# Expert weights in DRAM as quarters of 128 rows of 4 KB, and a spare 896-byte tile in the feed-forward stage

## The chip, the cores and the metric

The kernel runs on one core of one Trainium2 chip. The metric is the device time of the run in microseconds (us). All data are float32; the engines are TensorE (PE in the rows, PEld for its weight loads), VectorE (DVE), ScalarE (ACT), GpSimd (POOL) and SyncE (SP, which here issues most of the DMA transfers).

## The reference

Three layers follow each other on 8 x 3072 tokens of width 256: a spectral filter along the sequence, a mixture of 8 experts with one expert per token, and a dense feed-forward layer.

```
X = np.fft.rfft(x, axis=1)                       # x: (8, 3072, 256)
y = np.fft.irfft(X * (filt_r + 1j * filt_i)[None], n=3072, axis=1)
x = y.reshape(8 * 3072, 256)
logits = normalised(x) @ normalised(expert_emb).T / tau
expert_idx = argmax(logits); gate_w = softmax(logits)[expert_idx]
for e in range(8):                               # w1[e]: (256, 1024), w2[e]: (1024, 256)
    out[mask_e] = gate_w[mask_e] * (maximum(x[mask_e] @ w1[e], 0) @ w2[e])
h = out @ w_in                                   # (24576, 2048)
result = (h - tanh(h)) @ w_out
```

## The kernel before

**Stages.** The filter stage (`fft_phase`) computes the Fourier transforms as matrix products, batch after batch, routes each token, and scatters each token's row with GpSimd's indirect DMA (L393) into `region`, a DRAM buffer with one area per expert. The expert stage (`Moe`) then makes *visits*: one visit takes 384 or 256 consecutive rows of one expert's area through both matrices of that expert and writes the result to `x2T` in DRAM. The feed-forward stage (`ff_phase`, lines from L1200 on) comes last and fills more than half of the run.

**Visits.** The first visits (256 rows) run inside the filter stage, on experts that have enough rows by then. From visit `KV` on come the large ones (384 rows each), and then 13 small ones (256 rows each) for what is left over of each expert. One visit has four steps `b2`. In a step TensorE does 12 matmuls of the first matrix (`up`, L982) and, two steps late, 12 of the second (`down`, L1015); ScalarE and VectorE between them turn the first product into a high and a low part (`relu`, L992 and L993). Each engine works through its queue in order.

**Weights of an expert.** The matrices come in four *quarters* of 512 KB: quarters 0 and 1 are the two halves of `w1`, quarters 2 and 3 those of `w2`. One buffer, `raw`, holds one expert. In step `b2` of visit v the kernel first splits quarter `b2` of the next visit's expert into high and low parts (`split`: ScalarE L929, then VectorE or GpSimd L930), and then issues on SP the load of the same quarter for visit v+2 (`wload`, which calls `quarter`, L834 and L838). So a quarter that is reloaded has about one visit in which to arrive. From the second expert visit of the late part on, a load carries a condition (`cond=`) and moves nothing where the expert does not change; the split is done in every visit. The very first expert's weights go to a buffer of their own, `eraw`, inside the filter stage.

In `quarter` the source of a `w1` quarter is a view with three dimensions: 4 groups, 32 rows, 1024 values. The source of a `w2` quarter has 128 rows, 4 pieces of 256 values each:

```
wv = self.w1[bass.ds(e, 1)].rearrange("o (i k j) f -> (o k) i j f", i=4, k=2)
wv = self.w2[bass.ds(e, 1)].rearrange("o (b p) d -> (o p) b d", p=128)
```

**Rows of a visit.** SP also loads the visit's rows `y` in four parts (L896), reads the visit's numbers with small register loads (L823), and stores the result (L1028, L1029). GpSimd scales the rows (`rows`, L943 and L944), VectorE transposes them (L953), ScalarE and VectorE split them (L960, L961). L943 waits for the scatters of L393 that GpSimd issued before it.

**Buffers of the feed-forward.** `ff_phase` opens pools in the part of SBUF that the visits used; a tile there waits for the last user of the bytes that it takes. Its first small tile, `gones`, is filled by ScalarE (L1224) ahead of all of ScalarE's feed-forward work.

Of the kernel before, what the change touches and what calls it, by code (L numbers as in the profile page):

```python
# [16 lines left out]
F32 = mybir.dt.float32  # L17
# [9 lines left out]
D = 256  # L27
S = 3072
E = 8
FE = 1024  # L30
# [28 lines left out]
def flat(t):  # L59
    return t.rearrange("p a b -> p (a b)")  # L60
# [58 lines left out]
def fft_phase(tc, K, x, fr, fn, fi, emb, tau, region, ids, base, NB, CAP, moe):  # L119
# [3 lines left out]
    with ExitStack() as es:  # L123
# [208 lines left out]
        def route(b, g, Y, ss, L):  # L332
# [36 lines left out]

            P = L[:, 8:].rearrange("p a (b c) -> p (a b c)", b=4).rearrange("p (a b c) -> p a b c", a=2, b=8)  # L370

            def count():
                nc.tensor.matmul(P[:, 0], tri, ohv, start=True, stop=True)
                nc.tensor.matmul(P[:, 1], ones, ohv, start=True, stop=True)

            def place():

                inc = rp.tile([128, 8, 8], F32, name="inc", bufs=1)
                nc.vector.tensor_tensor_scan(flat(inc), flat(mask), flat(P[:, 1]), 0.0, op0=ALU.mult, op1=ALU.add)
                a = rp.tile([128, 8, 8], F32, name="a8", bufs=1)  # L380
                nc.vector.tensor_tensor(a, inc, P[:, 1], op=ALU.subtract)
                nc.vector.tensor_tensor(a, a, P[:, 0], op=ALU.add)
                nc.vector.tensor_tensor(a, a, bc(base), op=ALU.add)
# [376 lines left out]
class Moe:  # L760
# [68 lines left out]

    def quarter(self, q, e, **kw):  # L830

        if q < 2:
            wv = self.w1[bass.ds(e, 1)].rearrange("o (i k j) f -> (o k) i j f", i=4, k=2)
            self.tc.nc.sync.dma_start(self.raw[0][:, q], wv[q], **kw)  # L834
        else:
            wv = self.w2[bass.ds(e, 1)].rearrange("o (b p) d -> (o p) b d", p=128)
            b = slice(4 * q - 8, 4 * q - 4)
            self.tc.nc.sync.dma_start(self.raw[1][:, b], wv[:, b], **kw)  # L838

    def fetch(self, q):  # L840

# [364 lines left out]
def ff_phase(tc, x2T, ids, out, weights, mx, N, X0, fits, again):  # L1206

    nc = tc.nc
# [2 lines left out]
    NG = 8 * NT  # L1211
    with ExitStack() as es:
        P = lambda name, bufs, **kw: es.enter_context(tc.tile_pool(name=name, bufs=bufs, reuse_waits="tile", **kw))
        cp = P("gc", 1)
        beta = cp.tile([128, 1], F32, name="beta")
        nc.vector.memset(beta, BETA)
# [255 lines left out]
        for t in range(NT + 1):  # L1472
            for e, q in queue.items():
                seen = {}
                for n in table(t)[e].split():
                    i = seen[n] = seen.get(n, -1) + 1
# [14 lines left out]
        r = nc.values_load(bigi, min_val=0, max_val=1, skip_runtime_bounds_check_because="0 or 1")  # L1491
# [80 lines left out]
def moe_again(tc, region, w1, w2, x2T, ids, cnt, NA, N, CAP):  # L1572

    nc = tc.nc
    with ExitStack() as es:
        P = lambda name, bufs, **kw: es.enter_context(tc.tile_pool(name=name, bufs=bufs, **kw))
        p, hb = P("ag", 1), P("agb", 2)
        hp, op, dp = P("agh", 2, space=PSUM), P("ago", 2, space=PSUM), P("agd", 1, space=DRAM)
        zero = p.tile([128, RW], F32, name="zero")
        nc.vector.memset(zero, 0.0)  # L1580
        for i in range(TV // 128 * E):
            e, r = divmod(128 * i, TV)
            nc.sync.dma_start(region[e * CAP + r : e * CAP + r + 128], zero)
        sc = moe_schedule(tc, p, cnt, moe_numbers(tc, p, CAP, NA), CAP)
        table = dp.tile([128, 4], I32, name="table")
        nc.sync.dma_start(table, sc)
        NT = TV // 32
        with tc.For_i(0, N // TV + E - 1, 1) as v:
            line = p.tile([1, 4], I32, name="line")
            nc.sync.dma_start(line, table[bass.ds(v, 1)])  # L1590
            val = lambda k, top: nc.values_load(line[:, k : k + 1], engines=[SP], min_val=0, max_val=top,
                                                skip_runtime_bounds_check_because="the schedule stays inside")
            row, col, e = val(0, 8 * CAP - TV), val(1, N), val(2, E - 1)
            raw1 = p.tile([128, 2, FE], F32, name="raw1")
            raw2 = p.tile([128, 8, D], F32, name="raw2")
            wv = w1[bass.ds(e, 1)].rearrange("o (i k j) f -> (o k) i j f", i=4, k=2)
            for k in range(2):
                nc.sync.dma_start(raw1[:, k], wv[k])
            nc.sync.dma_start(raw2, w2[bass.ds(e, 1)].rearrange("o (b p) d -> (o p) b d", p=128))
            w1h, w1l = [p.tile([128, 2, FE], F32R, name=n) for n in ("w1h", "w1l")]  # L1600
            w2h, w2l = [p.tile([128, 8, D], F32R, name=n) for n in ("w2h", "w2l")]
            for r, h, l in ((raw1, w1h, w1l), (raw2, w2h, w2l)):
                nc.scalar.activation(h, r, AF.Copy)
                nc.vector.tensor_tensor(l, r, h.bitcast(F32), op=ALU.subtract)
            y = p.tile([128, NT, 68], F32, name="y")
            rv = region[bass.ds(row, TV)].rearrange("(t j) c -> j t c", j=32)
            for i, c in enumerate(QUARTERS):
                o = i % 2 * 2
                nc.sync.dma_start(y[32 * i : 32 * i + 32, :, o : o + 66], rv[:, :, c : c + 66])
            for q in (32, 96):  # L1610
                nc.gpsimd.tensor_copy(y[q : q + 32, :, 0:1], y[q : q + 32, :, 66:67])
            ys, yt = [p.tile([128, 2 * TV], F32, name=n) for n in ("ys", "yt")]
            nc.gpsimd.tensor_tensor(ys.rearrange("p (k t c) -> p t k c", k=2, c=32),
                                    y[:, :, 2:66].rearrange("p t (k c) -> p t k c", k=2),
                                    y[:, :, 0:1].unsqueeze(3).to_broadcast([128, NT, 2, 32]), op=ALU.mult)
            it, it2 = [p.tile([32, 32], I32, name=n) for n in ("it", "it2")]
            nc.vector.memset(it, 0)
            nc.vector.tensor_copy(it[:, :NT], y[:32, :, 1:2].bitcast(I32).rearrange("p t o -> p (t o)"))
            nc.vector.transpose(yt, ys)
            nc.vector.transpose(it2, it)  # L1620
            yh, yl = [p.tile([128, 2, TV], F32R, name=n) for n in ("yh", "yl")]
            nc.scalar.activation(flat(yh), yt, AF.Copy)
            nc.vector.tensor_tensor(flat(yl), yt, flat(yh).bitcast(F32), op=ALU.subtract)
            out = [op.tile([128, 512], F32, name="o")[:, :TV] for _ in range(2)]
            for fb in range(8):
                h = hp.tile([128, 512], F32, name="h")[:, :TV]
                c = slice(128 * fb, 128 * fb + 128)
                n = 0
                for k in range(2):
                    for a, b in ((w1h, yh), (w1h, yl), (w1l, yh)):  # L1630
                        nc.tensor.matmul(h, a[:, k, c], b[:, k], start=n == 0, stop=n == 5)
                        n += 1
                hh, hl = [hb.tile([128, TV], F32R, name=n) for n in ("hh", "hl")]
                nc.scalar.activation(hh, h, AF.Relu)
                nc.vector.scalar_tensor_tensor(hl, h, 0.0, hh.bitcast(F32), op0=ALU.max, op1=ALU.subtract)
                for d in range(2):
                    c = slice(128 * d, 128 * d + 128)
                    for n, (a, b) in enumerate(((w2h, hh), (w2h, hl), (w2l, hh))):
                        nc.tensor.matmul(out[d], a[:, fb, c], b, start=fb == 0 and n == 0, stop=fb == 7 and n == 2)
            x2 = p.tile([128, 2, TV], F32, name="x2")  # L1640
            for d in range(2):
                nc.scalar.activation(x2[:, d], out[d], AF.Copy)
            nc.sync.dma_start(x2T[:, bass.ds(col, TV)].rearrange("(k p) n -> p k n", p=128), x2)
            nc.sync.dma_start(ids[bass.ds(col, TV)].rearrange("(t j) -> t j", j=32), it2[:NT])
# [48 lines left out]
def arrange(x, filt_r, filt_i, moe_expert_emb, moe_tau, moe_w1, moe_w2, moe2_w_in, moe2_w_out):  # L1693
    mats, bins = dft_constants()
    c = np.ascontiguousarray
    a = dict(mats)
    a["x"] = c(x)
    a["fr"] = c(filt_r[bins[0]]).reshape(2 * N2, NP * D)
    a["fn"] = c(filt_r[S // 2 :])
    a["fi"] = c(filt_i[np.concatenate([bins[0, :, : NP // 2], bins[0, :, NP // 2 :]])]).reshape(NK, NP // 2 * D)  # L1700
    a["emb"] = c(moe_expert_emb)
    a["tau"] = np.asarray(moe_tau).reshape(1, 1)
    a["w1"] = c(moe_w1)
    a["w2"] = c(moe_w2)
    a["w_in"] = c(moe2_w_in).view(np.int64)
    a["w_out"] = c(moe2_w_out).view(np.int64)
    return a
# [15 lines left out]
```

## Time and profile before

| | |
|---|---|
| median of 3 runs | 3803.2 us (3803.08 to 3803.39) |
| the profiled execution, its own time | 3800.12 us |
| its span, first to last instruction | 3798.3 us |
| TensorE busy (matmuls) | 3684.9 us, 97% of the span |
| granted TensorE clock, mean | 0.987 of full speed |

The profiled execution took 1.8 us more than its span, and the median of the runs lies 3.1 us above it. The busy share is an average over three very different stages, so the rows below are taken stage by stage. "Granted clock" 1.00 is 2.4 GHz, 0.5 is 1.2 GHz.

### The profile page before, as it was taken

Reading aid. Unit: us, or ns where it says so; the run is one execution under the profiler, and the core shown is the slowest. Engines: PE = TensorE matmul, PEld = TensorE weight load, DVE = VectorE, ACT = ScalarE, POOL = GpSimd, SP = SyncE. Lnnn points to the kernel's source line nnn. Section 1 sums busy time; section 2 is a strip of 40 time slices with the busy share of each in tenths; the row PEclk is TensorE's granted clock in tenths of the full one; section 3 lists DMA queues with packets and bytes.
Section 4 is the critical chain, followed back from the end, with each engine's and each line's share of the span. In section 5 each row is a group of like instructions: output and inputs, shape, how many; then the busy total and the mean of one; then the engine's idle time right before and its main releaser. Section 6 shows DMA issues by size and latency. Waiting matters only on the chain.

```text
span 3798.3 us, 67513 instructions
## 1 busy us (share of the span) xinstructions
PE 3684.9 (97%) x23860; PEld 3348.8 (88%) x23860; DVE 2701.0 (71%) x5090; ACT 2536.1 (67%) x4327; POOL 2273.3 (60%) x1597
## 2 busy tenths in 40 slices
PE   6999889999999999989999999999999999999998
PEld 3666568999999999978899999999999999999997
DVE  4788885777887787647666666666666666676666
ACT  3566655455555555546777777777777777777775
POOL 2476666344344434435677777777777777777765
PEclk8999999999999999999999999999999999999999
DMA  8999864423332232440000000000000000000000
GB/s 258 300 296 295 267 183 143 104 56 82 84 81 81 70 94 58 110 122 26 29 25 27 23 29 23 29 23 28 24 29 23 23 29 27 25 23 29 25 28 18
DMA packets 295829, 308.49 MB, mean 81 GB/s; under 512 B 150193, under 2 KB 236346, under 8 KB 295482
## 3 DMA queue, kind: packets, MB, share of 16 engines
q1 hardware_dynamic: 232634, 199.37, 19.5%
q10 hardware_dynamic: 44416, 53.77, 4.3%
q0 software_dynamic: 18432, 50.95, 3.7%
q8 instruction: 190, 3.11, 0.3%
q14 instruction: 157, 1.29, 0.1%
HBM read 277.22 MB, written 127.41 MB: 107 GB/s over the span
## 4 chain that ended last, share of the span: by engine, by line
PE 85%; DMA 5%; DVE 5%; issue 2%; ACT 1%; POOL 1%; SPq 0%; POOLq 0%; ACTq 0%; DVEq 0%
PE h L1296 24%; PE po L1300 19%; PE h L982 12%; PE o L1015 12%; PE po L1301 10%; DMA raw<-in_w 3%; PE z L270 2%; PE z L255 2%; PE z L228 1%; PE z L297 1%; PE h L1281 1%; DVE u L262 1%; DVE v L261 1%; DVE v L260 1%; DMA region<-Y,pi 1%
## 5 line engine op out<-in xcount | busy, mean ns | idle before, releaser
L1362 POOL TENSOR_TENSOR gl<-g,gh 128x1024 fp32r<-128x1024 f32 x383 | 924.3, 2414 | 556.2 <-ACT gh L1359 435.2
L1300 PE MATMUL po<-wo,gh 128*128 128x512 f32 x3072 | 1148.9, 396 | 0.0
L1301 PE MATMUL po<-wo,gl 128*128 128x256 f32 x3072 | 864.5, 281 | 0.0
L1345 ACT ACTIVATE u<-h 128x512 f32<-128x512 f32 x768 | 453.6, 598 | 320.0 <-PE h L1296 292.1
L1341 DVE TENSOR_TENSOR h<-h,A 128x256 f32<-128x256 f32 x736 | 317.8, 432 | 491.5 <-PE h L1296 347.4
L930 POOL TENSOR_TENSOR w2l<-raw,w2h 128x1024 fp32r<-128x1024 f32 x126 | 305.4, 2447 | 572.7 <-ACT w2h L929 556.2
L1300 PEld LDWEIGHTS po<-wo,gh 128*128 128x128 f32 x3072 | 580.1, 189 | 71.6
L1348 DVE SCALAR_TENSOR_TENSOR h<-h,u 128x512 f32<-128x512 f32 x768 | 527.4, 693 | 105.4 <-ACT u L1345 104.2
L1301 PEld LDWEIGHTS po<-wo,gl 128*128 128x128 f32 x3072 | 578.2, 188 | 1.1
L1356 DVE SCALAR_TENSOR_TENSOR g<-s,h 128x512 f32<-128x512 f32 x768 | 500.8, 682 | 19.1 <-ACT s L1351 7.6
L992 ACT ACTIVATE hh<-h 128x384 fp32r<-128x384 f32 (+1 forms) x496 | 247.3, 510 | 365.5 <-PE h L982 365.1
L1351 ACT ACTIVATE s<-u,beta 128x1024 f32<-128x1024 f32 x384 | 442.8, 1153 | 12.6 <-DVE g L1356 3.2
L1296 PE MATMUL h<-xh,Sh 128*128 128x256 f32 x1472 | 414.1, 281 | 2.7 <-DVE g L1356 2.7
L1296 PE MATMUL h<-xh,Sl 128*128 128x256 f32 x1472 | 414.6, 282 | 0.0
L1296 PE MATMUL h<-xl,Sh 128*128 128x256 f32 x1472 | 414.5, 282 | 0.0
L993 DVE SCALAR_TENSOR_TENSOR hl<-h,hh 128x384 fp32r<-128x384 f32 (+1 forms) x496 | 273.4, 569 | 188.4 <-ACT hh L992 186.9
L1359 ACT ACTIVATE gh<-g 128x1024 fp32r<-128x1024 f32 x383 | 402.4, 1051 | 7.1 <-DVE g L1356 5.7
L1015 PE MATMUL o<-hl,w2h 128*128 128x384 f32 (+1 forms) x1184 | 380.5, 321 | 13.2 <-DVE hl L993 13.2
L982 PE MATMUL h<-yh,w1h 128*128 128x384 f32 (+1 forms) x1184 | 382.9, 323 | 10.5 <-DVE hl L993 4.2
L1015 PE MATMUL o<-hh,w2h 128*128 128x384 f32 (+1 forms) x1184 | 379.7, 321 | 8.5 <-ACT hh L992 8.4
L982 PE MATMUL h<-yh,w1l 128*128 128x384 f32 (+1 forms) x1184 | 378.7, 320 | 1.1 <-DVE w1l L930 1.1
L1015 PE MATMUL o<-hh,w2l 128*128 128x384 f32 (+1 forms) x1184 | 379.6, 321 | 0.0
(284 smaller groups left out, 8677.1 us busy)
## 6 DMA issues: line engine op xcount, KB each, us to landing
raw<-in_w SPq DMA_DIRECT2D x256, 512.0 KB
xt<-in_x SPq DMA_DIRECT2D x48, 512.0 KB
z1d<-a ACTq DMA_DIRECT2D x96, 256.0 KB
A<-z1d SPq DMA_DIRECT2D x64, 384.0 KB
z3d<-b ACTq DMA_DIRECT2D x128, 192.0 KB
bt<-z3d SPq DMA_DIRECT2D x96, 256.0 KB
x<-x2T SPq DMA_DIRECT2D x47, 512.0 KB
y<-region SPq DMA_DIRECT2D x200, 99.0 KB
```

What stands on the lines that cost most here:

```text
L982: nc.tensor.matmul(h[j], p[:, k, c], q[:, k], start=n == 0, stop=n == 5)
L1015: nc.tensor.matmul(O[v][d], p[:, fb, c], q[:, j], start=fb == 0 and n == 0 and (d == 0 or size(v) == TV), stop=fb == 7 and n == 2 and (d = ...
L1296: nc.tensor.matmul(h, a[:, w], b, start=n == "M5" and a is ah and b is xh, stop=False, skip_group_check=True)
L1300: nc.tensor.matmul(po, gh[:, c], flat(wo[:, f]), start=begin, stop=False)
L1301: nc.tensor.matmul(po[:, :D], gl[:, c], wo[:, f, 0], start=False, stop=end)
L1341: nc.vector.tensor_tensor(B[n == "opc"][g % 2][:, first], B[1][g % 2][:, second], A5[g % 2], op=ALU.add)
L1345: nc.scalar.activation(U[g][:, f], B[f][g % 2], AF.Square)
L1348: nc.vector.scalar_tensor_tensor(h, h, Q3[2], U[g][:, f], op0=ALU.mult, op1=ALU.mult)
L1351: nc.scalar.activation(O[g], U[g], AF.Square, bias=beta)
L1356: nc.vector.scalar_tensor_tensor(Q[g][:, f], O[g][:, f], KAPPA, B[f][g % 2], op0=ALU.add, op1=ALU.mult)
L1359: nc.scalar.activation(G[g][0], Q[g], AF.Copy)
L1362: nc.gpsimd.tensor_tensor(G[g][1], Q.pop(g), G[g][0].bitcast(F32), op=ALU.subtract)
```

## The change

The host lays out the expert weights in another order before the launch: `w1` and `w2` become arrays of 8 experts x 2 quarters x 128 rows x 1024 values. A quarter is then one block of 512 KB whose row p holds the 4 KB that go to partition p, and both sides of each load are 128 rows of 4 KB. In `ff_phase` a pool with one tile of 896 bytes per partition is opened ahead of all others; nothing writes or reads it.

```
     def quarter(self, q, e, **kw):
-        if q < 2:
-            wv = self.w1[bass.ds(e, 1)].rearrange("o (i k j) f -> (o k) i j f", i=4, k=2)
-            self.tc.nc.sync.dma_start(self.raw[0][:, q], wv[q], **kw)
-        else:
-            wv = self.w2[bass.ds(e, 1)].rearrange("o (b p) d -> (o p) b d", p=128)
-            b = slice(4 * q - 8, 4 * q - 4)
-            self.tc.nc.sync.dma_start(self.raw[1][:, b], wv[:, b], **kw)
+        wv = (self.w1, self.w2)[q // 2][bass.ds(e, 1)].rearrange("o q p f -> (o q) p f")[q % 2]
+        d = self.raw[0][:, q] if q < 2 else flat(self.raw[1][:, 4 * q - 8 : 4 * q - 4])
+        self.tc.nc.sync.dma_start(d, wv, **kw)
...
         P = lambda name, bufs, **kw: es.enter_context(tc.tile_pool(name=name, bufs=bufs, reuse_waits="tile", **kw))
+        P("gz", 1).tile([128, 224], F32, name="spare")
         cp = P("gc", 1)
...
-    a["w1"] = c(moe_w1)
-    a["w2"] = c(moe_w2)
+    a["w1"] = c(moe_w1.reshape(E, 4, 2, 32, FE).transpose(0, 2, 1, 3, 4)).reshape(E, 2, 128, FE)
+    a["w2"] = c(moe_w2.reshape(E, 2, 4, 128, D).transpose(0, 1, 3, 2, 4)).reshape(E, 2, 128, 4 * D)
```

The same loads in `moe_again`, a fallback that runs only when the counts or the values of the run don't fit the main path, are changed alike.

No instruction of the main path is added, removed or moved on any engine. SP's queue in a small visit, from the load of quarter 1 to that of quarter 2, stood so before (the names in brackets are the semaphores that a row waits for):

```order
L834 DMA raw_5657<-in_w 128x1x1024 [waits DMAHW0_49,DVE_49]
L823 TENSOR_LOAD slresi
L1028 REGISTER_ALU
L1028 DMA x2T<-x_19006 128x2x256 [waits DMAHW1_49,Activation_49]
L1029 REGISTER_ALU
L1029 DMA ids<-it_18592 8x32 [waits DMAHW2_49]
L838 REGISTER_ALU x2
L838 ISA
L838 DMA raw_5658<-in_w 128x4x256 [waits DMAHW3_49,Pool_49]
```

The order and the waits are the same after the change; the shapes of the loads become 128x1024. On ScalarE one wait is new. The start of its feed-forward work before:

```order
L1025 ACTIVATE x_20257<-o 128x256 [waits DMAHW7_49,PE_49]
L1025 ACTIVATE x_20257<-o 128x256
L1224 ACTIVATE gones<-gone 128x128 [waits DVE_49]
L1345 ACTIVATE u<-h_20303 128x512 [waits PE_49]
L1345 ACTIVATE u<-h_20301 128x512 [waits PE_49]
```

and after:

```order
L1021 ACTIVATE x_20257<-o 128x256 [waits DMAHW7_49,PE_49]
L1021 ACTIVATE x_20257<-o 128x256
L1221 ACTIVATE gones<-gone 128x128 [waits SP_sequencer_49,DVE_49]
L1342 ACTIVATE u<-h_20307 128x512 [waits PE_49]
L1342 ACTIVATE u<-h_20305 128x512 [waits PE_49]
```

`gones` now lies on bytes that held the visits' numbers and so waits until SP has done its last register load (L823). A later tile of the same engine no longer has that wait.

## Rows read from the trace of the kernel before

**Rows 1.** The page: span, TensorE's busy time, granted clock in 40 slices.

```profile
span 3798.3 us, 67513 instructions
...
PE 3684.9 (97%) x23860; PEld 3348.8 (88%) x23860; DVE 2701.0 (71%) x5090; ACT 2536.1 (67%) x4327; POOL 2273.3 (60%) x1597
...
PEclk8999999999999999999999999999999999999999
```

**Rows 2.** Stretches: length; busy us of PE, PEld, DVE, ACT, POOL; clock, DMA, GB/s.

```profile
560.00:720.00 160.00, 152.59 (x1256) 141.57 (x1249) 96.82 (x305) 80.91 (x189) 81.13 (x91) 0.98 0.42 120
720.00:1545.00 825.00, 825.00 (x4765) 825.00 (x4765) 660.35 (x1247) 467.64 (x778) 345.93 (x250) 1.00 0.31 80
1557.00:1581.00 24.00, 24.00 (x202) 24.00 (x201) 17.08 (x24) 14.07 (x22) 13.80 (x11) 1.00 0.43 106
1581.00:1712.00 131.00, 109.39 (x797) 105.78 (x796) 65.18 (x100) 60.42 (x92) 55.29 (x42) 0.91 0.44 116
1740.00:3798.00 2058.00, 2042.94 (x14056) 1893.91 (x14054) 1408.48 (x2512) 1566.47 (x2423) 1446.24 (x898) 1.00 0.09 25
```

**Rows 3.** ScalarE's groups in 1581 to 1712: busy, mean ns | idle before, releaser.

```profile
L929 ACT ACTIVATE w1h<-raw 128x1024 fp32r<-128x1024 f32 x17 | 18.0, 1056 | 55.1 <-DMA raw<-in_w 55.1
L929 ACT ACTIVATE w2h<-raw 128x1024 fp32r<-128x1024 f32 x17 | 17.8, 1045 | 0.0
```

**Rows 4.** ScalarE's timeline, two visits: start us, us, instruction, idle before.

```profile
1565.59 1.06 ACT L929 ACTIVATE w1h<-raw 128x1024 fp32r<-128x1024 f32 x1 [3.32 <-DMA raw<-in_w]
...
1582.19 0.58 ACT L992 ACTIVATE hh<-h 128x512 fp32r<-128x512 f32 x1
1590.01 1.06 ACT L929 ACTIVATE w1h<-raw 128x1024 fp32r<-128x1024 f32 x1 [7.24 <-DMA raw<-in_w]
...
1596.23 1.06 ACT L929 ACTIVATE w1h<-raw 128x1024 fp32r<-128x1024 f32 x1 [4.67 <-DMA raw<-in_w]
```

**Rows 5.** SP's timeline beside it: both `w1` quarters are issued in this row.

```profile
1579.98 2.06 SPq L834 DMA_DIRECT2D raw<-in_w  x2
```

**Rows 6.** Two short stretches, columns as in rows 2.

```profile
2.50:7.50 5.00, 2.23 (x3) 1.18 (x4) 4.88 (x10) 0.14 (x1) 5.00 (x1) 1.00 0.80 305
1592.00:1593.40 1.40, 0.20 (x1) 0.20 (x2) 1.11 (x4) 0.00 (x0) 0.00 (x0) 0.79 0.25 102
```

**Rows 7.** Transfers on the chain that ended last: start us, us.

```profile
1.20 3.94 DMA xt<-in_x
...
19.13 5.50 DMA xt<-in_x
...
609.46 16.96 DMA raw<-in_w
...
1581.43 14.77 DMA raw<-in_w
```

**Rows 8.** GpSimd's timeline around the load at 609, and one visit later.

```profile
620.49 0.99 POOL L393 DMA_INDIRECT region<-Y,pi  x1 [0.30 <-DMA region<-Y,pi]
626.28 0.44 POOL L943 COPY y<-y 32x8 f32<-32x8 f32 x2 [4.80 <-issue]
...
641.53 0.45 POOL L943 COPY y<-y 32x8 f32<-32x8 f32 x2 [1.72 <-DMA region<-Y,pi]
```

**Rows 9.** TensorE's waits in 560 to 720, then 440 to 560: total, times, longest.

```profile
PE h L982 <- DVE hl L993: 4.2, 2, 3.9
PE h L982 <- DVE it L947: 3.3, 1, 3.3
...
PE z L270 <- POOL u L263: 8.9, 9, 3.5
```

**Rows 10.** The feed-forward's start: `gones` on ScalarE, SP's last register load.

```profile
1738.62 0.31 ACT L1224 ACTIVATE gones<-gone 128x128 fp32r<-128x128 f32 x1 [0.90 <-DVE gone L1222]
...
L823 SPq TENSOR_LOAD <-slresi x1: 689/689/689, 1730.9 to 1730.9; - x1
```

**Rows 11.** GpSimd's costliest groups, feed-forward and visits: busy, mean ns | idle.

```profile
L1362 POOL TENSOR_TENSOR gl<-g,gh 128x1024 fp32r<-128x1024 f32 x383 | 924.3, 2414 | 556.2 <-ACT gh L1359 435.2
...
L930 POOL TENSOR_TENSOR w2l<-raw,w2h 128x1024 fp32r<-128x1024 f32 x126 | 305.4, 2447 | 572.7 <-ACT w2h L929 556.2
```

More of the change, by code (lines that the diff above doesn't have):

```diff
@@ L1595, in moe_again @@
             raw2 = p.tile([128, 8, D], F32, name="raw2")
-            wv = w1[bass.ds(e, 1)].rearrange("o (i k j) f -> (o k) i j f", i=4, k=2)
             for k in range(2):
-                nc.sync.dma_start(raw1[:, k], wv[k])
-            nc.sync.dma_start(raw2, w2[bass.ds(e, 1)].rearrange("o (b p) d -> (o p) b d", p=128))
+                for w, r in ((w1, raw1[:, k]), (w2, flat(raw2[:, 4 * k : 4 * k + 4]))):
+                    nc.sync.dma_start(r, w[bass.ds(e, 1)].rearrange("o q p f -> (o q) p f")[k])
             w1h, w1l = [p.tile([128, 2, FE], F32R, name=n) for n in ("w1h", "w1l")]
```

## The prediction

> **What bounds the kernel now.** I read the page first, then a table by stage, then who waits for whom in the stage that stood out, and last the timelines there.
>
> The page shows TensorE busy for 97% of a span of 3798.3 us, and a granted clock that falls below 9 tenths in only one of forty slices [rows 1]. So a change to transfers can give back at most the idle time and the slow clock of a few places. The table by stage finds them. In the large visits, 720 to 1545, TensorE is busy for 825.00 of 825 us at clock 1.00: no load is waited for there. In the feed-forward, 1740 to 3798, it is busy for 2042.94 of 2058 us. The small visits stand out: from 1557 to 1581 TensorE runs 202 matmuls in 24 us without a gap, but from 1581 to 1712 only 797 in 131 us, 21.6 us of it idle, at a mean clock of 0.91 [rows 2].
>
> What it waits for there is two steps away. ScalarE stands idle for 55.1 us ahead of its 17 splits of `w1` quarters, all of it released by the transfer of `raw`; ahead of the splits of `w2` quarters it never waits [rows 3]. Behind the waiting split, in the same queue, stands `hh`, without which the second products can't start; so TensorE runs dry. The timeline shows both what is tolerated and what isn't: a wait of 3.32 us at 1565 lies inside the stretch without a gap, waits of 7.24 and 4.67 us at 1582 to 1596 lie where TensorE starves [rows 2, 4].
>
> Why the transfer is late: SP issues both `w1` quarters from 1579.98 on [rows 5], and the chain that ended last holds a piece of 14.77 us of this transfer [rows 7]. While nothing but `w1` is moving (1592.0 to 1593.4), the 16 DMA engines are busy for 0.25 of the time at 102 GB/s; when the first tiles of `x` are loaded, in pieces of 128 rows of 4 KB as the changed loads will be, they are busy for 0.80 at 305 GB/s [rows 6]. A quarter of the engines is 4 of 16, the size of the outermost dimension of the `w1` view.
>
> **The change part by part**, against the profiled execution's own 3800.1 us.
>
> *The `w1` loads in the small visits.* At the pace of the undisturbed stretch, 24/202 = 0.1188 us for a matmul, the 797 matmuls take 94.7 us, not 131: 36.3 us are lost. The other way round: 21.6 us idle and (1 - 0.91) x 131 = 11.8 us of slow clock make 33.4 [rows 2]. I take 35. How much comes back hangs on how long the new load takes. The trace holds no load of this shape in the small visits, so I bound it by the tiles of `x`: 3.94 us alone, 5.50 us among the filter's full traffic [rows 7]. Quarter 0 was issued at 1579.98, and ScalarE came to its split when `hh` ended, at 1582.77: 2.8 us later. The split would then wait 1.1 us, or 2.7 at the upper bound, and 3.32 was tolerated [rows 4, 5, 7]. I take the shorter, since this stage moves 116 GB/s [rows 2] and is far from full. Quarter 1 follows about 1.4 us behind and is asked for about as much later. So TensorE loses nothing there: **-35 us** (bounds -20 and -36.3). What is late next is nothing that the rows show: the other engines did the same splits in the stretch without a gap.
>
> *The `w1` load at 609*, for the expert that the filter's last batches choose. The transfer takes 16.96 us [rows 7], and GpSimd pays for it: its copy at 626.28 waits 4.80 us after the scatter at 620.49, where one visit later the same wait is 1.72 us [rows 8]; the scatters' packets share the four engines. That is 3.1 us of GpSimd's queue, which TensorE's gap of 3.9 us at 656 follows through the scaled rows, their transpose and split [rows 9]; a gap this long is followed by a slow clock (0.98 in the stretch, 160 x 0.02 = 3.2 us) [rows 2]. VectorE is paced by TensorE in part of the way, so not all comes through: **-3 us** (0 to -6).
>
> *The first expert's loads, from 465 on.* TensorE's largest waits there are for GpSimd's sums, 8.9 us in nine pieces, not for a load [rows 9]: 0 (at best -3.5, the longest piece).
>
> *The `w2` loads and those of the large visits.* The split never waited for the first, and TensorE never for the second [rows 2, 3]: 0. Their cover is the visit's length; if it were gone, they would now take as long as a `w1` load.
>
> *The spare tile.* No work of its own. `gones` now waits for SP's last register load, which ended near 1731.6, while ScalarE did not reach `gones` before 1737: 5 us of cover, and behind it waits all of ScalarE's feed-forward work [rows 10]. With the visits shorter, both ends move together. All tiles of the stage shift by 896 bytes. What that does, the rows can only hint at: GpSimd's like instruction took 2414 ns on these tiles and 2447 ns on the visits' tiles elsewhere, over groups in which it idles 556 us and more [rows 11]. I take 0; if each of the 383 became 33 ns longer, 12.6 us would be hidden in that idle time.
> The Trainium skill, SBUF — State Buffer, section "Who interferes with whom", also names only the port pair of VectorE and GpSimd and no address as a cause of contention; by it the sum is the same. The rows differ by 1.4% between addresses, so they agree as far as they go.
>
> The sum: 3800.1 - 35 - 3 = 3762. The median lies 3.1 us above this execution, so I predict **3765 us**.
>
> **The rivals.**
>
> *Half of it.* The wait may stay, shorter, if the load arrives late for another reason: SP's queue holds quarter 0 until 1579.98 already [rows 5], and it meets rows, results and the other quarters of the same visit. It decides at 2.8 + 3.3 = 6.1 us from issue to split; today the split of quarter 0 starts 10.0 us after the issue [rows 4, 5]. For it: only the 5.50 us in full traffic, near the limit. With half the loss left: 3765 + 17 = 3782.
>
> *The change doesn't do what it says*: the pace of `w1` comes from something else than the number of engines, say the place in DRAM. Then nothing moves, 3803. Against it: the share of 0.25 [rows 6].
> The Trainium skill, DMA: Bandwidth & Descriptors, section "Why a DMA increments its semaphore by 16 and not by 1", has a rule for this: a transfer uses the largest number up to 16 that divides the outermost sizes of both sides. For 4 and 128 that gives 4 engines, for 128 and 128 all 16; the trace agrees with its 4. By the rule the 14.77 us would become an estimated 3.7 us and the 35 us come back whole; by a limit in DRAM they stay lost.
>
> *Slower*: the shifted tiles slow TensorE's own reads in the feed-forward, where it is busy 99% of the time and has no cover. From 38/2043 = 1.9% on, the gain is gone; at 3% the run ends near 3765 + 61 = 3826 [rows 2]. Nothing in the rows speaks for such a size.
>
> **How the numbers follow.** The forecast, with 3756 to 3772 as its own range (terms at their bounds), gets 0.72; half of it 0.18; no change 0.05; slower 0.05. A measurement of this kernel can tell about 0.2%, 7.6 us, from no change. The first case lies wholly beyond it on the fast side, and the second nearly so: 0.90 faster, 0.05 same, 0.05 slower. The range 3754 to 3784 holds the first case and the larger part of the second.
>
> **What would show it.** In the changed trace ScalarE's wait for `raw` should fall from 55.1 us to below 15, with no single wait above 3.5; the small visits should run through at some 202 matmuls in 24 us and clock 1.00; while only `w1` moves, the DMA share should be well above 0.25; GpSimd's copy near 626 should wait about 2 us, and TensorE's gap near 656 shrink below 2; the large visits and the feed-forward should keep their 825 and 2058 us. I am wrong if the `w1` loads still take over 6 us, if TensorE starves in the small visits for another releaser, or if the feed-forward's length moves by more than 5 us.

## The result and the profile after

The changed kernel takes 3759.9 us (median of 4 runs, 3758.88 to 3763.88), the kernel before beside it 3803.3 us (3803.08 to 3804.88): ratio 0.9887, 95% interval 0.9870 to 0.9904. That is 43.4 us less; forecast were 38.

The profiled execution spans 3758.0 us, 40.3 less than that of before [rows 1]. First the page of the changed kernel:

```profile
span 3758.0 us, 67515 instructions
...
PE 3670.4 (98%) x23860; PEld 3340.8 (89%) x23860; DVE 2701.9 (72%) x5090; ACT 2537.8 (68%) x4327; POOL 2277.2 (61%) x1597
...
PEclk8999989999999999999999999999999999999999
```

The table by stretches, columns as in [rows 2]; the last row is a short stretch in which nearly only `w1` moves, to be read beside [rows 6]:

```profile
560.00:720.00 160.00, 155.21 (x1288) 143.15 (x1287) 99.14 (x317) 84.42 (x200) 81.87 (x96) 0.99 0.43 126
720.00:1545.00 825.00, 825.00 (x4769) 825.00 (x4768) 660.68 (x1246) 468.79 (x779) 344.61 (x250) 1.00 0.29 80
1557.00:1581.00 24.00, 24.00 (x203) 24.00 (x202) 17.50 (x25) 15.31 (x24) 14.21 (x10) 1.00 0.36 104
1581.00:1703.00 122.00, 122.00 (x1019) 122.00 (x1018) 83.78 (x118) 72.42 (x111) 68.66 (x47) 1.00 0.45 132
1706.00:3758.00 2052.00, 2036.68 (x14059) 1893.90 (x14057) 1408.37 (x2513) 1567.58 (x2424) 1447.91 (x898) 1.00 0.09 26
1580.50:1583.50 3.00, 3.00 (x28) 3.00 (x27) 1.98 (x3) 3.00 (x5) 1.32 (x1) 1.00 0.82 247
```

Nearly all that the weights gave lies in the small visits: TensorE is busy for 122 of 122 us at clock 1.00, 1019 matmuls at 0.1197 us each, where it had 21.6 us of idle time and a clock of 0.91 [rows 2]. While `w1` moves, the engines are busy for 0.82 of the time at 247 GB/s; it was 0.25 at 102 [rows 6]. ScalarE's groups in the small visits (busy, mean ns | idle before) no longer wait for `raw`; its 55.1 us of waiting are gone [rows 3]:

```profile
L925 ACT ACTIVATE w2h<-raw 128x1024 fp32r<-128x1024 f32 x24 | 25.6, 1067 | 0.0
L925 ACT ACTIVATE w1h<-raw 128x1024 fp32r<-128x1024 f32 x22 | 23.1, 1051 | 0.0
```

The visit that answers to [rows 4, 5]: SP's timeline with the issue of both `w1` quarters, then ScalarE's with their splits (the change gives all four quarters one line, L834).

```profile
1579.23 1.77 SPq L834 DMA_DIRECT2D raw<-in_w  x2
```

```profile
1584.85 1.05 ACT L925 ACTIVATE w1h<-raw 128x1024 fp32r<-128x1024 f32 x1
1587.17 0.60 ACT L988 ACTIVATE hh<-h 128x512 fp32r<-128x512 f32 x1 [1.27 <-PE h L978]
1587.67 1.05 ACT L925 ACTIVATE w1h<-raw 128x1024 fp32r<-128x1024 f32 x1
```

ScalarE comes to the split 5.6 us after the issue and finds the data there; what it waits for now is TensorE (`hh<-h`).

Around the load at 609, GpSimd's copies and then TensorE's waits in 560 to 720, to be read beside [rows 8, 9]:

```profile
612.09 0.45 POOL L939 COPY y<-y 32x8 f32<-32x8 f32 x2 [2.83 <-issue]
629.41 0.45 POOL L939 COPY y<-y 32x8 f32<-32x8 f32 x2 [1.92 <-DMA region<-Y,pi]
```

```profile
PE h L978 <- DVE it L943: 3.3, 1, 3.3
PE h L978 <- DVE hl L989: 1.5, 1, 1.5
```

GpSimd's wait of 4.80 us is now 1.92, and TensorE's wait of 3.9 us for the split is 1.5; the one of 3.3 us for the slots is as it was. The stretch between the same two instructions around that wait, in the kernel before and in the changed one (columns as in [rows 2]):

```profile
640.30:675.71 35.41, 31.26 (x246) 30.85 (x245) 25.25 (x81) 13.54 (x25) 23.50 (x28) 0.95 0.35 102
```

```profile
647.14:678.18 31.04, 29.51 (x246) 29.31 (x245) 25.74 (x81) 13.32 (x25) 21.15 (x26) 1.00 0.39 113
```

ScalarE's start of the feed-forward, beside [rows 10]:

```profile
1705.37 0.31 ACT L1221 ACTIVATE gones<-gone 128x128 fp32r<-128x128 f32 x1 [0.90 <-DVE gone L1219]
```

`gones` waits for VectorE as before, 0.90 us, and not for SP.

**Where the 40.3 us came from.** ScalarE runs the same instructions in the same order in all kernels of this study, so each execution can be cut at the start of the same ScalarE instructions; in the kernel before they start at 536.88, 692.27, 1556.34 and 1737.05 us. The last column runs to the end of the span, and the times are those of one profiled execution each.

| kernel | to 537 | 537 to 692 | large visits | small visits | feed-forward |
|---|---|---|---|---|---|
| before | 536.9 | 155.4 | 864.1 | 180.7 | 2061.2 |
| changed | 542.0 | 152.8 | 864.1 | 145.0 | 2054.2 |
| difference | +5.1 | -2.6 | 0.0 | -35.7 | -7.0 |

Two of these were not in the prediction: the feed-forward is 7.0 us shorter, and the first part, in which only the first expert's load at its end is changed, is 5.1 us longer in this pair of executions.

### The profile page after: what moved, and what is told of

Its sections match the earlier page's. It is cut to its first block, busy times and chain, and to the rows that moved or that the text cites. A ratio compares the mean times of both kernels' runs of the same rounds, so it can differ in the third digit from the quotient of the medians.

```text
span 3758.0 us, 67515 instructions
## 1 busy us (share of the span) xinstructions
PE 3670.4 (98%) x23860; PEld 3340.8 (89%) x23860; DVE 2701.9 (72%) x5090; ACT 2537.8 (68%) x4327; POOL 2277.2 (61%) x1597
## 4 chain that ended last, share of the span: by engine, by line
PE 81%; DVE 1%; issue 0%; ACT 0%; POOL 0%; DMA 0%; POOLq 0%; DVEq 0%
PE h L1293 24%; PE po L1297 19%; PE o L1011 14%; PE h L978 14%; PE po L1298 10%; PE h L1278 1%; DVE hl L989 0%; DMA region<-Y,pi 0%; DVE w2l L926 0%; POOL ys L940 0%; DVE g L1353 0%; DVE h L1345 0%; DVE yl L957 0%; DVE Sl L1398 0%; DVE mx L1022 0%
## 5 line engine op out<-in xcount | busy, mean ns | idle before, releaser
L1298 PE MATMUL po<-wo,gl 128*128 128x256 f32 x3072 | 864.1, 281 | 0.0
L978 PE MATMUL h<-yl,w1h 128*128 128x384 f32 (+1 forms) x1184 | 376.8, 318 | 0.0
```

The source lines that it names most:

```text
L978: nc.tensor.matmul(h[j], p[:, k, c], q[:, k], start=n == 0, stop=n == 5)
L1298: nc.tensor.matmul(po[:, :D], gl[:, c], wo[:, f, 0], start=False, stop=end)
```

## The experiments

My theory: the loads of `w1` came late because a transfer whose outermost size is 4 uses 4 of 16 engines; and the 7.0 us in the feed-forward come from the 896 bytes alone. The rivals: what counts in the layout is the contiguous block, or `w2`'s fewer packets; and the feed-forward's gain is chance or the placement of data in DRAM. "Feed-forward" and "small visits" are the columns of the table above throughout.

**1. The change without the spare tile** (`no_spare`).

```diff
-        P("gz", 1).tile([128, 224], F32, name="spare")
```

> The changed kernel without the spare tile. Both weight layouts stay. First theory: the 896 bytes alone make the feed-forward 7.0 us shorter, through the 512-column matmuls of its second product (231.1 instead of 233.6 ns from one to the next). Then this run takes 3760 + 7 = 3767 us, the feed-forward 2061 us from its first matmul of 48, and the interval is 233.6 ns again. Rival: the shorter feed-forward has nothing to do with the tile (a different placement of data in DRAM, or chance): 3760 us, 2054 us, 231 ns. In both cases the small visits keep their 33 us or more.

Measured: 3764.8 us, ratio to before 0.9895 (0.9880 to 0.9910); feed-forward 2061.4 us, small visits 145.0. The first theory holds.

**2. The kernel before with the spare tile alone** (`spare_only`).

```diff
+        P("gz", 1).tile([128, 224], F32, name="spare")
         cp = P("gc", 1)
```

> The kernel before with nothing but the spare tile added. First theory: 3803.3 - 7.0 = 3796 us, feed-forward 2054 us, 231 ns between 512-column matmuls; the small visits lose their 36 us as before. Rival: 3803 us, 2061 us. A third reading, that ScalarE's new wait ahead of its first feed-forward work costs something, would show as a start of the feed-forward that is more than 0.5 us later after the last visit's matmul.

Measured: 3797.4 us against 3804.65, ratio 0.9982 (0.9973 to 0.9991); feed-forward 2054.1, small visits 180.6. So the tile is worth 7 us whatever the layout, in the time of 11 runs as in the trace. The third reading is out: `gones` starts 1.56 us after the beginning of the last column, where it started after 1.57 in the kernel before.

**3. `w1` alone laid out anew** (`w1_only`): as the change, but `w2` and its loads as before, and no tile. The cut shows the load; the host's order of `w1` is that of the change.

```diff
-            wv = self.w1[bass.ds(e, 1)].rearrange("o (i k j) f -> (o k) i j f", i=4, k=2)
+            wv = self.w1[bass.ds(e, 1)].rearrange("o q p f -> (o q) p f")
             self.tc.nc.sync.dma_start(self.raw[0][:, q], wv[q], **kw)
```

> The kernel before with w1 alone laid out anew; w2 is loaded as 512 packets of 1 KB as before, and there is no spare tile. First theory: w1 carries all that the layout gives, 35.7 us in the small visits and 4 us at the load at 609: 3803.3 - 40 = 3763 us, with 5 us either way for the filter stage; ScalarE waits for no w1 quarter in the small visits. Rival: w2's small packets cost the small visits something too (they share the engines with w1 and the rows): TensorE idles some us there, and the run takes 3768 us or more beyond what the filter stage explains.

Measured: 3765.6 us, ratio 0.9899 (0.9883 to 0.9914); small visits 145.0, the same as in run 1, which differs from it by `w2` alone. ScalarE's groups of the small visits in this run:

```profile
L929 ACT ACTIVATE w2h<-raw 128x1024 fp32r<-128x1024 f32 x24 | 25.5, 1064 | 0.0
L929 ACT ACTIVATE w1h<-raw 128x1024 fp32r<-128x1024 f32 x22 | 23.1, 1052 | 0.0
```

`w2`'s layout gives nothing that the trace or the time shows.

**4. Eight and sixteen groups** (`groups8`, `groups16`): the changed kernel with `w1` stored so that a quarter is again no contiguous block.

```diff
+            wv = self.w1[bass.ds(e, 1)].rearrange("o (i k j) f -> (o k) i j f", i=8, k=2)[q]
```

(with i=16 in the second; the host's order follows).

> The changed kernel with w1 stored so that a quarter is 8 groups of 16 rows of 4 KB, 128 KB apart from the other quarter's groups: the outermost size of the load is 8, the packets are still 4 KB. First theory: the number of engines is the outermost size. A pair of w1 quarters then takes about half of 14.8 us, 7.4 us, the DMA share while only w1 moves is 0.5, ScalarE waits some 2.4 us for most quarters (5.0 us from issue to split where 2.8 us are free, and 8.1 where 5.6 are), which is under the 3.32 us that was tolerated: 3760 to 3765 us. Rival 1: it is the contiguous block of 512 KB that counts, not the number of engines: a pair takes 14 us still, TensorE starves again, 3795 us. Rival 2: the tolerance is smaller than I read: the loads take 7.4 us, but TensorE idles at each pair, 3770 to 3780 us.

> The changed kernel with w1 in 16 groups of 8 rows of 4 KB, the groups 64 KB apart, so that a quarter is again no contiguous block, but the outermost size is 16. First theory, the number of engines is all: the small visits and the last large ones take 145.0 us as with 128 rows in one block, ScalarE waits for no quarter. Rival, the contiguous block matters too: some wait remains, 145.5 us or more (8 groups: 151.1 us, 4 groups: 180.7).

Measured with 8 groups: 3765.1 us, ratio 0.9898 (0.9883 to 0.9913); small visits 151.1. With 16 groups, one run: 3761.1 us, small visits 145.0 and no wait, the same as one block of 128 rows. So the size of the outermost dimension decides, and the contiguous block is worth nothing here. ScalarE's group and its single waits with 8 groups, and the stretches:

```profile
L928 ACT ACTIVATE w1h<-raw 128x1024 fp32r<-128x1024 f32 x23 | 24.3, 1057 | 25.7 <-DMA raw<-in_w 25.7
```

```profile
1590.68 1.06 ACT L928 ACTIVATE w1h<-raw 128x1024 fp32r<-128x1024 f32 x1 [0.21 <-DMA raw<-in_w]
1595.42 1.06 ACT L928 ACTIVATE w1h<-raw 128x1024 fp32r<-128x1024 f32 x1 [2.13 <-DMA raw<-in_w]
...
1640.81 1.06 ACT L928 ACTIVATE w1h<-raw 128x1024 fp32r<-128x1024 f32 x1 [3.58 <-DMA raw<-in_w]
1646.18 1.06 ACT L928 ACTIVATE w1h<-raw 128x1024 fp32r<-128x1024 f32 x1 [3.83 <-DMA raw<-in_w]
...
1679.63 1.06 ACT L928 ACTIVATE w1h<-raw 128x1024 fp32r<-128x1024 f32 x1 [2.62 <-DMA raw<-in_w]
1684.20 1.06 ACT L928 ACTIVATE w1h<-raw 128x1024 fp32r<-128x1024 f32 x1 [3.03 <-DMA raw<-in_w]
```

```profile
1564.00:1589.00 25.00, 25.00 (x210) 25.00 (x210) 18.12 (x26) 16.30 (x25) 15.52 (x11) 1.00 0.45 125
1589.00:1715.00 126.00, 122.46 (x1002) 121.65 (x1001) 80.61 (x115) 69.46 (x108) 64.04 (x47) 0.99 0.50 126
1586.20:1587.70 1.50, 1.50 (x15) 1.50 (x15) 1.27 (x2) 1.50 (x3) 0.00 (x1) 1.00 0.43 127
```

The wait per loaded quarter is 25.7/10 = 2.6 us, as forecast (2.4), and at the start of a pair the DMA share is 0.43, between 0.25 and 0.82. But the second rival is right in part: 6.1 us are lost, 3.5 of them idle, and the clock is 0.99 over the 126 us. Of the five pairs of waits TensorE absorbed three, whose two waits add up to 2.3, 5.0 (with a single one of 3.24) and 5.3 us. Behind the pair of 3.58 and 3.83 us it stood still for 2.1 us (the longer gap, 1.7 us, from 1648), and behind the last, 2.62 and 3.03 us, for 1.5. Each of these last two waits is shorter than the 3.32 us that I had taken as tolerated. So the limit does not hold for a wait by itself: the waits of one visit add up. The last pair also came 13 us after the one before it, the others 25; whether that is why it cost more than the pair of 5.3 us is not shown.

**5. The size of the spare tile.** Five kernels, the changed one with another tile, one profile each. `gh`, the weights that TensorE loads in the second product, lies, by the kernel's allocation, 32 bytes past a multiple of 256 without a tile and 160 past one with 896 bytes. `Sh` and `Sl`, weights of the first product, and the split rows that lie beside them in `cp` begin on the same number of bytes past 256 as `gh` in all of these.

```diff
-        P("gz", 1).tile([128, 224], F32, name="spare")
+        P("gz", 1).tile([128, 32], F32, name="spare")
```

> The changed kernel with a spare tile of 128 bytes instead of 896. Read from the profile: the feed-forward from the last visit's result on, 2061.2 to 2061.5 us without a tile, 2053.6 to 2054.2 with 896 bytes, and the interval of the 512-column matmuls, 233.6 or 231.1 ns. 896 is 7 x 128, so 128 bytes give the same place within 256 bytes. First theory, that the place within 256 bytes decides: 2054 us and 231 ns. Rival, that the distance itself or a place within a larger block decides: 2061 us, or a value of its own.

> The changed kernel with a spare tile of 512 bytes: all tiles of the stage are moved, but their place within 256 and within 512 bytes is that of no tile. First theory (place within 256 bytes decides): 2061 us, 233.6 ns. Rival, that any move does it (the tiles against those that stay, such as the output weights): 2054 us.

> The changed kernel with a spare tile of 448 bytes, half of 896: a place within 256 bytes 64 bytes past that of 896 bytes (448 = 256 + 192, 896 = 768 + 128). First theory: a value of its own, between or beyond 2054 and 2061 us. If it is 2061 or 2054 exactly, there are two classes of places, not a gradual effect.

> The changed kernel with a spare tile of 224 bytes: the weights of the second product then begin on a multiple of 256 bytes (they lie 32 bytes past one without a tile, 160 with 896 or 128 bytes, 224 with 448). If full alignment is best: below 2053 us and below 231 ns. If the three places measured so far lie on a smooth curve (32: 2061, 160: 2053.5, 224: 2071), 0 lies between 224 and 32, some 2065 us.

> The changed kernel with a spare tile of 96 bytes: the weights of the second product begin 128 bytes past a multiple of 256. On a smooth curve this lies between 32 (2061) and 160 (2053.5), near 2055 us. If a multiple of 128 bytes is a class of its own: below 2053 us.

Two more move only a part of the tiles: `late_128` has the tile behind `cp` (the constants, with `Sh`, `Sl` and one of the two sets of split rows) and ahead of the pools of `gh` and `gl`; `early_128` has 128 bytes ahead of `cp` and 384 behind it. So `Sh` lies 32 past 256 in the first and 160 in the second.

```diff
-        P("gz", 1).tile([128, 224], F32, name="spare")
         cp = P("gc", 1)
...
+        P("gz", 1).tile([128, 32], F32, name="spare")
         xp = P("gx", 2)
```

> The changed kernel with a spare tile of 128 bytes opened behind the pool of the constants: the tiles of the first product (the sums of the input matrix, the split rows) stay where they are without a tile, and only the pools behind it move, among them the two parts of the activated values that TensorE loads as weights of the second product. First theory, that the place of these weights within 256 bytes decides: 2053 to 2054 us, 231 ns. Rival, that the operands of the first product decide: 2061 us, 233.6 ns.

> The changed kernel with a spare tile of 128 bytes ahead of the constants and a second one of 384 bytes behind them: the constants (among them the sums of the input matrix and the split rows) move by 128 bytes, the pools behind them by 512, which alone changed nothing. The counterpart of the run that moved only the pools behind (2057.3 us, 4 of the 7.6 us that a move of all tiles by 128 bytes gives). If the two parts add up: 2061.2 - 3.8 = 2057 to 2058 us. If the gain hangs on how the two groups lie to each other: 2061 us or slower.

Measured (TensorE was busy throughout 2000 to 3600 us at clock 1.00 in each; the matmuls there are counted in the table by stretches. The last two columns add up TensorE's time from each matmul's start to the next, in us over the feed-forward, by the product that the matmul belongs to):

| tile, bytes | time, one run | `gh` past 256 | feed-forward | matmuls in 1600 us | first product | second product |
|---|---|---|---|---|---|---|
| 0 (`no_spare`) | 3764.8 (median) | 32 | 2061.4 | 11167 | 959.7 | 1084.1 |
| 512 | 3767.5 | 32 | 2061.2 | 11167 | 960.1 | 1083.2 |
| 896 (the change) | 3759.9 (median) | 160 | 2054.2 | 11210 | 959.3 | 1077.3 |
| 128 | 3761.0 | 160 | 2052.6 | 11212 | 959.0 | 1076.2 |
| 224 | 3768.6 | 0 | 2059.1 | 11173 | 962.3 | 1079.4 |
| 96 | 3772.1 | 128 | 2067.1 | 11125 | 963.8 | 1085.9 |
| 448 | 3775.7 | 224 | 2071.4 | 11099 | 970.8 | 1083.3 |
| 128 behind `cp` (`late_128`) | 3760.7 | 160 | 2057.3 | 11184 | 962.6 | 1077.2 |
| 128 ahead of `cp`, 384 behind (`early_128`) | 3767.1 | 32 | 2061.6 | 11160 | 964.2 | 1080.0 |

The feed-forward column is the one to compare: single times also hold the scatter of the filter stage (the kernel before took 3800.0 to 3810.4 us beside these runs).

The place within 256 bytes reproduces the time: 0 and 512 bytes agree to 0.2 us and to the matmul, 128 and 896 to 1.6 us, over different shifts. But no simple rule follows: a smooth curve and full alignment both missed (2059 and 2067 where I gave 2065 or under 2053, and 2055 or under 2053), and the two parts don't add up (moving the pools behind alone gives about 4 of the 7 to 8 us, moving the constants alone nothing). The last two columns show where the time sits. With 896 and 128 bytes the gain is the second product's, 6.8 and 7.9 us. With 448 bytes the loss is the first product's, 11.1 us, and the second is no slower than without a tile. The two runs that move a part are each faster in the second product (6.9 and 4.1 us) and slower in the first (2.9 and 4.5), so the "nothing" of the constants is two effects that cancel. The groups in the page (busy, mean ns) of before, of the change and of the tile of 448 bytes; the `wo` lines are the second product, the `Sl` line is one group of the first:

```profile
L1300 PE MATMUL po<-wo,gh 128*128 128x512 f32 x3072 | 1148.9, 396 | 0.0
L1301 PE MATMUL po<-wo,gl 128*128 128x256 f32 x3072 | 864.5, 281 | 0.0
...
L1296 PE MATMUL h<-xh,Sl 128*128 128x256 f32 x1472 | 414.6, 282 | 0.0
```

```profile
L1297 PE MATMUL po<-wo,gh 128*128 128x512 f32 x3072 | 1142.7, 395 | 0.0
L1298 PE MATMUL po<-wo,gl 128*128 128x256 f32 x3072 | 864.1, 281 | 0.0
...
L1293 PE MATMUL h<-xh,Sl 128*128 128x256 f32 x1472 | 413.8, 281 | 0.0
```

```profile
L1297 PE MATMUL po<-wo,gh 128*128 128x512 f32 x3072 | 1151.0, 398 | 0.0
L1298 PE MATMUL po<-wo,gl 128*128 128x256 f32 x3072 | 862.1, 281 | 0.0
...
L1293 PE MATMUL h<-xh,Sl 128*128 128x256 f32 x1472 | 416.7, 283 | 0.0
```

From one start to the next, averaged over the trace's starts in some 1600 us, the 512-column matmul takes 233.6 ns without a tile, 231.1 with 896 or 128 bytes and 235.4 with 448; 3072 x 2.5 ns are 7.7 us, the gain with 896 bytes and a little more (the 256-column matmul of the second product takes 119.0 ns instead of 118.7). The moving operand of the 512-column matmul, `wo`, lies in a pool that does not move; `gh` does.

## Why the prediction was right, and where it was not

*What bounds the kernel, and the small visits: right.* I took 35 us with bounds of 20 and 36.3, and 35.7 came back; the pace is that of the undisturbed stretch, 0.1197 us a matmul against 0.1188. One working number was off on the safe side: I read 2.8 us from issue to split in a visit that was itself disturbed. In the even rhythm it is 5.6 us, so the split does not wait at all where I had 1.1 us. "Half of it" therefore never came near. The limit that I set for it, 3.32 us for a wait, was misread all the same: ahead of that wait the first split of the visit had not waited at all, and with 8 groups TensorE ran dry behind two waits of 2.62 and 3.03 us in one visit.

*The engines: right*, and shown by 4, 8 and 16: 180.7, 151.1 and 145.0 us. The rival that the pace comes from the place in DRAM falls with the 16 groups that are no block.
The Trainium skill, DMA: Bandwidth & Descriptors, section "Why a DMA increments its semaphore by 16 and not by 1", counts the engines by the outermost sizes; the three times agree with it.

*The load at 609: mechanism right, size not settled.* GpSimd's wait was to fall to about 2 us and TensorE's gap below 2: they measure 1.92 and 1.5. GpSimd's wait is 4.5 to 4.8 us in the three kernels with 4 or 8 engines and 1.75 to 2.44 us in all eleven with 16. TensorE's gap measures 3.95 and 3.96 us in the two kernels with 4 engines, 2.6 with 8, and 0.9 to 1.7 in all eleven with 16. But the stretch from 537 to 692 shows little of it: 155.4 and 157.3 us with 4 engines and 157.3 with 8, 152.2 to 157.0 (mean 154.8) in the eleven with 16. The -3 I gave is -2.6 in the pair of profiles and -1.6 between the means, no more than the scatter. Part of the scatter lies ahead of the load: its first piece, up to the instruction that starts at 580 in the kernel before, takes 43.2 to 46.7 us at a granted clock of 0.84 to 0.96. The piece with the gap alone (640 to 676 before) takes 35.4 us in both kernels with 4 engines and 34.1 with 8; with 16 it takes 31.0 to 31.3 in four kernels, the changed one among them, and 34.0 to 34.9 in the other seven. So it gives 4.4 us in this pair and 0.5 to 1.4 in most others; why these fall into two groups is open.

*Large visits, `w2`: right*, nothing. The large visits take 864.1 us in all kernels but `spare_only` (865.4), and the runs with and without `w2`'s layout have the same small visits. The first fetch, also put at nothing, can't be read: its stage up to 537 scatters by 6.2 us over the profiles, more than the 3.5 that it had at best.

*The spare tile: wrong.* The step that failed is "I take 0": I looked for the effect on GpSimd, where the rows had a hint, and for ScalarE's wait, whose cover held (7.5 us in the changed kernel). It acts on TensorE, whose matmuls I allowed to change only in the rival that ends slower. That rival's mechanism was real: tiles moved by 448 bytes cost 10 us against no tile, by 896 they give 7. Its size was not the 1.9% that it needed; what was seen reaches from -0.4 to +0.5% of the feed-forward. By the prediction's own sign, a feed-forward that moves by more than 5 us, it was wrong here.
The Trainium skill, SBUF — State Buffer, section "Who interferes with whom", names no address among the causes of contention; the runs show that the place of tiles changes the time by up to 18.8 us (2052.6 to 2071.4).

*The sum.* 3800.1 - 35.7 - 2.6 - 7.0 + 5.1 = 3759.9, the profiled execution's own time (3759.8). The +5.1 is scatter of the filter stage: the same instructions up to 537 took 536.9 to 543.1 us over the fourteen profiles, `spare_only` with before's own weights 541.1, and the profile of before was the shortest of all. The two terms of the forecast, -38, measured -38.3, and the change without the tile, 3764.8 us, comes out at the 3765 forecast. That the second term's part of it agrees so well is luck, since its scatter is as large as it is. Against the medians, 5 us too high, it is the missing tile term that remains. The range of 3756 to 3772, called that of the terms at their bounds, is not their sum: the bounds as given make 3757 to 3783.

## What to carry to other kernels

When a load of a regular shape is slow, count the engines first: the DMA share while it moves alone tells it (0.25 here), and an outermost size of 16 or of 128 was enough (no size above 8 other than these was tried); a contiguous block brought nothing more. What late weights cost is read in the stage with the shortest rounds, and its cure can be read from the undisturbed stretch of the same stage. Before a difference of half a per cent in a matmul-bound stage is put down to an edit, check whether the edit moved the stage's tiles; a spare tile or two of other sizes shows it.

## What the hardware showed that I had not expected

The start address of SBUF tiles changes the spacing of matmuls that are bound by nothing else: 11099 to 11212 in 1600 us at clock 1.00, 1%, with the same instructions. It repeats to the matmul when tiles move by 512 bytes. Both products of the stage respond, and not alike: over the nine kernels the first takes 959.0 to 970.8 us, the second 1076.2 to 1085.9. The place of `gh` alone does not give it: 128 bytes behind `cp` and 128 ahead of everything leave `gh` on the same bytes and differ by 4.7 us, of which 3.6 lie in the first product, whose own tiles in `cp` differ. Which operand's place counts, and against which other access, of TensorE or of another engine, is open. Shifts of 32, 64 and 160 bytes were not tried.
